# A new order for the front of an attention kernel with a feed-forward behind it: last queries' scores in a score tile, tail keys as 64x64 products, copies changed between two engines, loads by head

## The chip, the cores and the metric

The kernel runs on one core of a Trainium2 chip. The core's engines each run their own queue of instructions in order: TensorE (PE: matrix products; its weight loads are listed as PEld), ScalarE (ACT: functions of single elements, such as the exponential, and copies), VectorE (DVE: element-wise products and copies), GpSimd (POOL: here it issues most loads) and SyncE (SP: here it issues stores, small loads and transposes by DMA). Matrix products write into PSUM, which is cut into banks; ScalarE and VectorE read them from there into SBUF. The metric is the device time of one execution in microseconds, as the median of several runs; lower is better.

## The reference

Attention over 8 batches of 8 heads, 576 positions and 64 dimensions per head, with a bias that depends on the distance of two positions alone, followed by a feed-forward without biases, from 512 to 2048 and back, with a leaky ReLU.

```
scores = scale * (q @ k.T) + bias_table[bucket(|i - j|), head]
attn   = softmax(scores)
x      = (attn @ v)            # (8 * 576) rows x 512
out    = leaky_relu(x @ w_in, 0.01) @ w_out
```

The bucket is constant from a distance of 128 on.

## The kernel before

Two heads make a pair; there are 32 pairs, n = 0 to 31, four to a batch (n_pairs = 4). Every engine's order is the order of the program text (a manual schedule), so the text below is the schedule.

For a pair, q and k are turned (positions from partitions to columns): transpose_q and transpose_k make twelve small PE transposes into a PSUM bank of the pool "m" (two banks), from which a copy writes qt or kt in SBUF. transpose_k also calls apart, which makes a block-diagonal copy of the last 64 keys of both heads. Pairs above 8 are turned by a DMA on SP's queue instead (turn_by_dma), for which pair_rows gathers the rows on VectorE.

Scores are computed with the keys on the partitions, in six units u. Units 0 to 3 (u < NJ) are 128 keys each against the first 512 queries, both heads side by side in a score tile of two banks (pool ps_s, two tiles). Unit 4 (u == NJ) holds those four blocks of keys against the last 64 queries, in the two banks o0 and o1 of the pool ps_o, in which the value products accumulate too. Unit 5 is the last 64 keys (tail keys) of both heads against all 576 queries. qk_mm(n, u) issues the products and exp(n, u, ps) lets ScalarE write the exponentials into at (units 0 to 4) or at4 (unit 5); score(n, u) is both. The maximum isn't subtracted. The bias enters as a factor behind the exponential: band(n, u) multiplies, on VectorE, the columns near the diagonal by rows of hk or hk4, which the program makes at the start from the table (through a row in DRAM, u_row, loaded back by SP's DMAs).

av_tails(n) and av(n, e) multiply with the values, which carry a column of ones, so that the sums stand beside the products; a reciprocal and a product on VectorE give opair. x_transposes(n) turns opair into xT, the input of the feed-forward, by PE and a copy, or by a DMA for later pairs.

The feed-forward works on tiles of 512 rows. ffn_in makes one group: four products of 128x512 into a bank of "m", from which leaky writes gt, on ScalarE in one pass, or, where by_vector is set, on VectorE in two (0.01 times the input into low, then the maximum). ffn_out multiplies back. A planner by counts decides how many groups each pair takes in (plan, groups_of, slot, moe, moe_block). The first tile of 512 rows is complete behind pair 3, so that the first groups stand in the loop of pair 4.

The order around the change: spins (products of zeros, to keep PE occupied), the turns of pair 0, its first scores, then a loop over n = 0 to 3 in which the scores of pair n, the value products of pair n - 1, and the turns of pair n + 1 are interleaved; then pair 4 written out by hand with its first four groups; then one loop over n = 5 to 32. In that loop the tail keys' scores (unit 5) come near the end of a pair, behind nearly all of its groups, and each next pair begins with the products of its units 0 and 1. Loads go through POOL: load_qk(b, h0, h1) is one DMA for q and one for k, load_v_head one head of values, load_v_part one block of 128 positions of several heads, load_v_tail the last 64 positions; loads(n), called from begin(n), issues those that belong to a pair. The values' tiles, q and k of two batches are held at a time.

## Time and profile before

| what | value |
|---|---|
| runs | 377.9, 378.34, 379.27 us (median 378.34) |
| the profiled execution's own time | 378.19 us |
| its span, first to last instruction | 376.4 us |
| TensorE clock granted | 1.0 |
| PE busy | 361.4 us (96%) |
| ScalarE, VectorE, POOL busy | 239.6, 201.8, 77.1 us |
| first feed-forward product | 34.29 us from the span's start |

A row of a timeline gives the start in microseconds, the duration, the engine, the line of the kernel, the operation, "output<-inputs" by the names in the program, partitions x elements, and how many of a kind follow one another (x4); a bracket at its end tells how long the engine stood idle before it, and what ended that. The duration of a merged row is the time that the records cover; since an instruction starts before the record of the one ahead has ended, the distance of two starts is what one takes of the queue. A row of the windows gives a stretch of the span, its length, and the busy time of each engine in it. PE's records are modelled, so that a busy PE need not be at its peak.

### The profile page before, as it was taken

The page shows a single profiled execution, that of the slowest core. Times are in us where ns is not written, and L with a number is a line of the kernel's source. Part 1 is how long each engine was busy: PE and PEld are TensorE (multiplying, and loading weights), DVE is VectorE, ACT ScalarE, POOL GpSimd, SP SyncE. Part 2 cuts the span into 40 slices and gives each one's busy share as a digit, 9 for nine tenths or more (in the row PEclk, how much of TensorE's full clock was granted, in tenths as well). Part 3 has the DMA queues.
Part 4 walks back from the last instruction along what each step waited for, and adds up shares of the span by engine and source line. Part 5 has one row for each costly group of instructions (what it writes and reads, how often), then busy time and mean ns, then how long its engine had stood idle before and what let it go on. Part 6 is the DMA issues. An engine that isn't in the chain of part 4 may idle for free.

```text
span 376.4 us, 8586 instructions
## 1 busy us (share of the span) xinstructions
PE 361.4 (96%) x3501; PEld 186.0 (49%) x3556; DVE 201.8 (54%) x510; ACT 239.6 (64%) x376; POOL 77.1 (20%) x118
## 2 busy tenths in 40 slices
PE   6879999999999999999999999999999999999995
PEld 2455555554455555555545545555555544444442
DVE  4689687777657666666755666655553300200221
ACT  5898777568856787777866666777777255055000
POOL 8772431233023303330323033100000000000000
PEclk9999999999999999999999999999999999999999
DMA  8999999997699959996998699433131000110212
GB/s 104 184 202 182 206 199 136 158 185 121 77 119 157 147 80 125 150 156 84 145 117 127 76 132 117 78 78 78 47 47 45 30 28 2 57 54 2 81 61 84
DMA packets 104352, 40.07 MB, mean 106 GB/s; under 512 B 83184, under 2 KB 98808, under 8 KB 104312
## 3 DMA queue, kind: packets, MB, share of 16 engines
q0 software_dynamic: 53696, 18.36, 47.1%
q1 hardware_dynamic: 50472, 21.02, 28.5%
q8 instruction: 28, 0.46, 0.5%
q10 hardware_dynamic: 144, 0.13, 0.1%
q14 instruction: 12, 0.10, 0.1%
HBM read 37.68 MB, written 9.45 MB: 125 GB/s over the span
## 4 chain that ended last, share of the span: by engine, by line
PE 85%; DMA 4%; ACT 4%; DVE 3%; issue 1%; SPq 1%; another core or an unknown queue 1%; DVEq 0%; ACTq 0%
PE pm L449 32%; PE pm L424 30%; PE ps_o L376 10%; PE ps_s L316 8%; DMA hk<-u_row 3%; PE ps_s L319 1%; PE ps_o L365 1%; ACT at L329 1%; ACT gt L435 1%; DVE opair L380 1%; DMA u_row<-ub 1%; SPq L199 1%; PE ps_tx L398 1%; PE ps_q L309 1%
## 5 line engine op out<-in xcount | busy, mean ns | idle before, releaser
L435 ACT ACTIVATE gt<-pm 128x512 bf16<-128x512 f32 x138 | 82.6, 603 | 88.4 <-PE pm L424 87.5
L424 PE MATMUL pm<-xT,w_in_sb 128*128 128x512 bf16 x543 | 136.4, 379 | 2.0 <-ACT gt L435 0.2
L449 PE MATMUL pm<-w_out_sb,gt 128*128 128x512 bf16 x555 | 130.9, 379 | 1.1
L329 ACT ACTIVATE at<-ps_s 128x1024 bf16<-128x1024 f32 x128 | 124.4, 1030 | 6.9 <-PE ps_s L316 6.8
L352 DVE TENSOR_TENSOR at<-at,hk 128x768 bf16<-128x768 bf16 (+3 forms) x160 | 71.4, 454 | 33.6 <-ACT at L332 19.8
L449 PEld LDWEIGHTS <-gt 128*128 128x128 bf16 x576 | 53.0, 98 | 60.6
L424 PEld LDWEIGHTS <-w_in_sb 128*128 128x128 bf16 x576 | 51.9, 98 | 53.9 <-issue 0.9
L467 DVE COPY y<-pm 128x512 f32<-128x512 f32 x33 | 22.8, 692 | 76.6 <-PE pm L449 76.6
L376 PE MATMUL ps_o<-vn,at 128*128 128x65 bf16 x1280 | 49.6, 194 | 0.0
L376 PEld LDWEIGHTS <-at 128*128 128x128 bf16 x1280 | 44.5, 98 | 9.0 <-issue 0.7
L316 PE MATMUL ps_s<-qt,kt 64*128 64x512 bf16 x256 | 40.4, 381 | 4.5 <-ACT at L329 3.2
L379 DVE RECIPROCAL rcp<-ps_o 128x5 f32<-128x5 f32 x64 | 12.3, 192 | 42.9 <-PE ps_o L376 42.7
L380 DVE TENSOR_TENSOR opair<-ps_o,rcp 128x320 bf16<-128x320 f32 x64 | 31.5, 492 | 3.3
L620 POOL COPY tick<-opair 1x1 bf16<-1x1 bf16 x18 | 4.6, 256 | 134.1 <-DVE opair L380 134.1
L119 POOL DMA_DIRECT2D vn<-in_v_dram x32 | 29.4, 923 | 9.9 <-PE pm L424 3.6
L316 PEld LDWEIGHTS <-kt 64*128 64x128 bf16 x256 | 8.5, 94 | 31.1 <-issue 23.6
L336 ACT ACTIVATE at<-ps_s 128x576 bf16<-128x576 f32 x32 | 21.9, 683 | 0.2 <-PE ps_s L320 0.2
L332 ACT ACTIVATE at<-ps_q 128x256 bf16<-128x256 f32 x64 | 21.6, 403 | 0.5 <-PE ps_q L309 0.4
L459 ACT COPY y<-pm 128x256 f32<-128x256 f32 x1 | 0.4, 372 | 27.5 <-DVE y L459 27.5
L298 DVE COPY kt<-tu 128x576 bf16<-128x576 bf16 x23 | 15.5, 675 | 0.0
L294 DVE COPY qt<-tu 128x576 bf16<-128x576 bf16 x23 | 15.0, 651 | 0.0
L112 POOL DMA_DIRECT2D qn<-in_q_dram x18 | 13.9, 773 | 3.6 <-DMA vn<-in_v_dram 1.0
(59 smaller groups left out, 177.5 us busy)
## 6 DMA issues: line engine op xcount, KB each, us to landing
out_dram<-y SPq DMA_DIRECT2D x35, 256.0 KB, 2.3
qn<-in_q_dram POOLq DMA_DIRECT2D x14, 288.0 KB, 5.5
kn<-in_k_dram POOLq DMA_DIRECT2D x14, 288.0 KB, 6.2
vn<-in_v_dram POOLq DMA_DIRECT2D x28, 128.0 KB, 6.2
w_in_sb<-in_moe_w_in_dram POOLq DMA_DIRECT2D x2, 1024.0 KB, 13.0
w_out_sb<-in_moe_w_out_dram POOLq DMA_DIRECT2D x2, 1024.0 KB, 16.3
qn<-in_q_dram POOLq DMA_DIRECT2D x4, 144.0 KB, 4.1
kn<-in_k_dram POOLq DMA_DIRECT2D x4, 144.0 KB, 4.3
```

The lines of the kernel that those rows point to most:

```text
L119: nc.gpsimd.dma_start(out=vn[b % NBUF][:, c, h0:h1, 0:D], in_=v[b, h0:h1, c * P : (c + 1) * P, :].rearrange("h s d -> s h d"),)
L316: nc.tensor.matmul(ps[:, e, :], lhsT=kt[r, u * P : (u + 1) * P], rhs=qt[r, 0:512], start=True, stop=True)
L329: nc.scalar.activation(at[:, :, u, 0:512], ps, AF.Exp, scale=scale)
L332: nc.scalar.activation(at[:, e, :, 512:S], ps[e][:, 0 : NJ * SL].rearrange("p (c i) -> p c i", i=SL), AF.Exp, scale=scale)
L336: nc.scalar.activation(at4[:, 0:S], ps.rearrange("p e i -> p (e i)")[:, 0:S], AF.Exp, scale=scale)
L352: nc.vector.tensor_tensor(out=o, in0=o, in1=m, op=ALU.mult)
L376: nc.tensor.matmul(ps[:, ic, :], lhsT=at[:, o : o + P], rhs=vn[b % NBUF][:, c, 2 * p + e, :], start=False, stop=(ic == NJ and c == NJ - 1))
L380: nc.vector.tensor_tensor(out=opair[:, :, e * D : (e + 1) * D], in0=ps[:, :, 0:D], in1=rcp.to_broadcast([P, NJ + 1, D]), op=ALU.mult)
L424: nc.tensor.matmul(pm, lhsT=w_in_sb[:, c, f * P : (f + 1) * P], rhs=xT[c][:, t0 : t0 + TT], start=(c == 0), stop=(c == n_cc - 1))
L435: nc.scalar.activation(g, pm, AF.Prelu, bias=0.0, scale=1.0, alpha=0.01)
L449: nc.tensor.matmul(pm, lhsT=gt[:, f, ts * P : (ts + 1) * P], rhs=w_out_sb[:, f, :], start=(f == 0), stop=(f == n_fc - 1))
L467: nc.vector.tensor_copy(out=y, in_=pm)
```

## The change

The loop over pairs 0 to 3 is written anew: pair 0 and the first steps of pair 1 stand ahead of a loop over n = 1 to 3, in which the turns of q and k of the next pair stand together, ahead of the scores of unit 2. For pairs below 4, unit 4 goes to a score tile and is one pass of ScalarE in place of two; unit 5 is made by four products with 64 rows and 64 columns, head by head, and apart isn't called. Copies of q are on ScalarE for pairs 0, 3 and 4 and on VectorE for all others (before: ScalarE for pairs 0 to 4); copies of the turned output are on ScalarE for pairs 0 to 2 (before: VectorE). Values of heads 4 to 7 of batch 0 are loaded head by head, q and k of batch 1 in three parts, of which the last is issued in loads(0), behind the values of batch 1.

In the loop over n = 5 to 32 a branch is added for pairs in which the planner has groups of the first projection alone and fewer than six of them (room["only"]): no group in the second slot, band(n, 1) later, unit 5 ahead of the last two groups, the last bands between the two halves of the group that VectorE finishes. The turns ahead by DMA are a function of their own, turn_ahead, called from begin where the next pair is turned by DMA, and otherwise behind the first value products.

```diff
--- before.py
+++ after.py
@@ -225,10 +225,13 @@
     load_qk(0, 6, H)
     load_v_head(0, 2)
     load_v_head(0, 3)
-    load_qk(1, 0, H // 2)
-    load_v_part(0, range(NJ), 4, H)
+    load_v_head(0, 4)
+    load_v_head(0, 5)
+    load_qk(1, 0, 2)
+    load_v_head(0, 6)
+    load_v_head(0, 7)
     clear_v(nc.gpsimd, 1)
-    load_qk(1, H // 2, H)
+    load_qk(1, 2, 4)
 
     def load_w_in(half):
         o = slice(half * (DF // 2), (half + 1) * (DF // 2))
@@ -290,17 +293,33 @@
 
     def transpose_q(n):
         qt = qts[n] = qt_pool.tile([P, S], BF16, name="qt")
-        copy = nc.scalar.copy if n <= n_pairs else nc.vector.tensor_copy
+        copy = nc.scalar.copy if n == 0 or n_pairs - 1 <= n <= n_pairs else nc.vector.tensor_copy
         copy(out=qt[:, 0:S].rearrange("p (r c) -> p r c", c=NC), in_=turned_pair(n, 0))
 
     def transpose_k(n):
         kt = kts[n] = kts_[n % 2]
         nc.vector.tensor_copy(out=kt[:, 0:S].rearrange("p (r c) -> p r c", c=NC), in_=turned_pair(n, 1))
-        apart(kt)
+        if n >= n_pairs:
+            apart(kt)
 
     def qk_mm(n, u):
 
         qt, kt = qts[n], kts[n]
+        if n < n_pairs and u >= NJ:
+            ps = ps_s_pool.tile([P, 2, 512], FP32, name="ps_s")
+            if u == NJ:
+                for c in range(NJ):
+                    for e in range(2):
+                        r = slice(e * D, (e + 1) * D)
+                        nc.tensor.matmul(ps[:, e, c * SL : (c + 1) * SL], lhsT=kt[r, c * P : (c + 1) * P],
+                                         rhs=qt[r, 512:S], start=True, stop=True)
+                return ps
+            for half, cols in ((0, slice(0, 512)), (1, slice(512, S))):
+                for e in range(2):
+                    r = slice(e * D, (e + 1) * D)
+                    nc.tensor.matmul(ps[e * SL : (e + 1) * SL, half, 0 : cols.stop - cols.start],
+                                     lhsT=kt[r, NJ * P : S], rhs=qt[r, cols], start=True, stop=True)
+            return ps
         if u == NJ:
             ps = [ps_o_pool.tile([P, 512], FP32, name="ps_q", tag=f"o{e}") for e in range(2)]
             for c in range(NJ):
@@ -327,6 +346,10 @@
         at, at4 = at_view(n), at4_[n % 2]
         if u < NJ:
             nc.scalar.activation(at[:, :, u, 0:512], ps, AF.Exp, scale=scale)
+        elif u == NJ and n < n_pairs:
+            nc.scalar.activation(at[:, :, :, 512:S],
+                                 ps[:, :, 0 : NJ * SL].rearrange("p e (c i) -> p e c i", i=SL),
+                                 AF.Exp, scale=scale)
         elif u == NJ:
             for e in range(2):
                 nc.scalar.activation(at[:, e, :, 512:S],
@@ -396,7 +419,8 @@
         ps = ps_m_pool.tile([P, 8 * P], BF16, name="ps_tx", tag="m")
         for ic in range(NJ + 1):
             nc.tensor.transpose(ps[:, ic * P : (ic + 1) * P], in_=opair[:, ic, :], identity=ident)
-        nc.vector.tensor_copy(out=xT[p][:, b * S : (b + 1) * S], in_=ps[:, 0:S])
+        copy = nc.scalar.copy if n < n_pairs - 1 else nc.vector.tensor_copy
+        copy(out=xT[p][:, b * S : (b + 1) * S], in_=ps[:, 0:S])
 
 
     gts = {}
@@ -425,11 +449,13 @@
                              start=(c == 0), stop=(c == n_cc - 1))
         return pm
 
-    def leaky(T, f, pm, by_vector=False):
+    def leaky(T, f, pm, by_vector=False, between=None):
         g = gts[T][:, f, :]
         if by_vector:
             low = low_pool.tile([P, TT], BF16, name="low")
             nc.vector.tensor_scalar(low, pm, 0.01, None, op0=ALU.mult)
+            if between is not None:
+                between()
             nc.vector.tensor_tensor(out=g, in0=low, in1=pm, op=ALU.max)
         else:
             nc.scalar.activation(g, pm, AF.Prelu, bias=0.0, scale=1.0, alpha=0.01)
@@ -521,16 +547,19 @@
         keep = min(n_fc, 4 * ((n - 1) // n_pairs)) if more <= N else 0
         return max(4, min(8, (have - keep) // (more - n)))
 
-    room = {"left": 0, "lead": False, "split": False, "keep": 0}
+    room = {"left": 0, "lead": False, "split": False, "only": False, "keep": 0}
 
     def plan(n):
         g = room["left"] = groups_of(n)
         room["lead"] = can("out") and g >= 8 and not can("in")
         room["split"] = can("out") and g < 8 and not can("in")
+        room["only"] = can("in") and not can("out") and g < 6
         room["keep"] = 4 if can("out") and not room["lead"] else 0
 
     def slot(second=False):
 
+        if room["only"] and second:
+            return
         if room["split"]:
             if second:
                 piece_out()
@@ -610,6 +639,7 @@
             load_w_in(0)
             load_v_part(1, range(NJ))
             load_v_tail(1)
+            load_qk(1, H // 2, H)
             load_w_in(1)
             load_w_out(0)
         elif n == 2:
@@ -632,6 +662,10 @@
         loads(n)
         if n_pairs + 1 < n + 1 < N and not by_dma(n + 1):
             pair_rows(n + 1)
+        if by_dma(n + 1):
+            turn_ahead(n)
+
+    def turn_ahead(n):
         for m in range(n + 2, min(n + AHEAD + 1, N)):
             if by_dma(m) and m - (AHEAD if m > 2 * n_pairs + 2 else 2) == n:
                 pair_rows(m)
@@ -646,39 +680,43 @@
     spin(2)
     score(0, 0)
     score(0, 1)
-    for n in range(n_pairs):
-        begin(n)
+    begin(0)
+    score(0, 2)
+    transpose_k(1)
+    transpose_q(1)
+    spin(3)
+    score(0, 3)
+    spin(3)
+    score(0, 5)
+    score(0, 4)
+    score(1, 0)
+    score(1, 1)
+    begin(1)
+    transpose_k(2)
+    spin(3)
+    for u in (0, 1, 2, 5, 4):
+        band(0, u)
+    score(1, 2)
+    transpose_q(2)
+    score(1, 3)
+    for n in range(1, n_pairs):
         if n > 1:
+            begin(n)
             band(n - 1, 5)
             band(n - 1, 4)
-        if n == 1:
-            for u in (0, 1, 2, 5, 4):
-                band(0, u)
-        if n == 0:
+            transpose_k(n + 1)
+            transpose_q(n + 1)
             score(n, 2)
-        transpose_k(n + 1)
-        if n < 2:
-            spin(3)
-        if n > 0:
-            score(n, 2)
-        if n == 1:
+        av_tails(n - 1)
+        av(n - 1, 0)
+        band(n, 0)
+        if n > 1:
             score(n, 3)
-        if n > 0:
-            av_tails(n - 1)
-            av(n - 1, 0)
-            band(n, 0)
-        if n != 1:
-            score(n, 3)
-        if n > 0:
-            av(n - 1, 1)
-        transpose_q(n + 1)
-        if n < 1:
-            spin(3)
+        av(n - 1, 1)
+        band(n, 1)
         score(n, 5)
-        if n > 0:
-            band(n, 1)
-            x_transposes(n - 1)
-            band(n, 2)
+        band(n, 2)
+        x_transposes(n - 1)
         score(n, 4)
         score(n + 1, 0)
         score(n + 1, 1)
@@ -722,13 +760,15 @@
             exp(n, 1, ps_b)
         av_tails(n - 1)
         av(n - 1, 0)
+        if live and not by_dma(n + 1):
+            turn_ahead(n)
         if live:
             band(n, 0)
         if more:
             transpose_q(n + 1)
         slot()
         av(n - 1, 1)
-        if live:
+        if live and not room["only"]:
             band(n, 1)
         if more:
             transpose_k(n + 1)
@@ -744,7 +784,24 @@
             finished(n - 1)
         if not live:
             break
+        if room["only"]:
+            band(n, 1)
         band(n, 2)
+        if room["only"]:
+            exp(n, 3, ps_b)
+            moe(2)
+            exp(n, 4, ps_c)
+            score(n, 5)
+            T, f = step("in")
+            room["left"] -= 1
+
+            def last_bands():
+                band(n, 5)
+                band(n, 4)
+
+            leaky(T, f, ffn_in(T, f), True, last_bands)
+            moe(room["left"])
+            continue
         block = moe_block()
         next(block)
         exp(n, 3, ps_b)
```

## The prediction

> **What bounds the kernel now.** I read the granted clock and the page's table of 40 slices first, then the windows of the front, then the timelines of ScalarE (ACT), VectorE (DVE) and TensorE (PE) there. The clock is 1.0 throughout, so no term below is a clock term.
>
> ```profile
> span 376.4 us, 8586 instructions
> PE 361.4 (96%) x3501; PEld 186.0 (49%) x3556; DVE 201.8 (54%) x510; ACT 239.6 (64%) x376; POOL 77.1 (20%) x118
> PE   6879999999999999999999999999999999999995
> ACT  5898777568856787777866666777777255055000
> PEclk9999999999999999999999999999999999999999
> ...
> 12.35:18.54 6.19, 5.04 (x98) 3.21 (x99) 4.93 (x14) 5.36 (x8) 4.21 (x8) 1.00 1.37 209
> 18.54:24.13 5.59, 4.50 (x105) 3.06 (x103) 4.56 (x13) 5.33 (x8) 2.83 (x4) 1.00 1.62 197
> 24.13:29.64 5.51, 4.55 (x107) 3.16 (x104) 4.55 (x13) 5.38 (x9) 4.11 (x6) 1.00 1.18 211
> 38.68:47.13 8.45, 8.24 (x105) 4.83 (x107) 5.68 (x13) 6.41 (x10) 3.18 (x5) 1.00 1.25 206
> 47.13:56.16 9.03, 8.41 (x106) 4.85 (x107) 7.19 (x18) 7.04 (x12) 3.24 (x5) 1.00 1.38 200
> ```
>
> Each window row gives its length, then the busy time of PE, weight loads, VectorE, ScalarE and POOL. Over the span PE is the bound, but not in the front: in the pairs that run from 18.54 and 24.13 ScalarE is busy 5.33 of 5.59 and 5.38 of 5.51 us, PE only 4.5. From pair 5 (38.68) on PE has 8.24 of 8.45. So a microsecond won or lost in the ScalarE-bound front moves everything behind it; once the change's stretch ends, at 56 us, the same PE work follows at its own pace, and nothing there absorbs a shift.
>
> ```profile
> 12.70 3.82 ACT L329 ACTIVATE at<-ps_s 128x1024 bf16<-128x1024 f32 x4
> 17.14 0.64 ACT L294 COPY qt<-ps_t 128x576 bf16<-128x576 bf16 x1 [0.63 <-PE ps_t L279]
> 17.68 0.66 ACT L336 ACTIVATE at<-ps_s 128x576 bf16<-128x576 f32 x1
> 18.74 0.66 ACT L332 ACTIVATE at<-ps_q 128x256 bf16<-128x256 f32 x2 [0.40 <-PE ps_q L309]
> 19.28 3.78 ACT L329 ACTIVATE at<-ps_s 128x1024 bf16<-128x1024 f32 x4
> 23.13 0.64 ACT L294 COPY qt<-ps_t 128x576 bf16<-128x576 bf16 x1
> 23.66 0.66 ACT L336 ACTIVATE at<-ps_s 128x576 bf16<-128x576 f32 x1
> 24.39 0.66 ACT L332 ACTIVATE at<-ps_q 128x256 bf16<-128x256 f32 x2
> 24.93 3.78 ACT L329 ACTIVATE at<-ps_s 128x1024 bf16<-128x1024 f32 x4
> 30.44 3.78 ACT L329 ACTIVATE at<-ps_s 128x1024 bf16<-128x1024 f32 x4
> ```
>
> Starts give what each operation really takes of the queue: a 128x1024 exponential (23.13-19.28)/4 = 0.96 us, a 576-wide q copy 23.66-23.13 = 0.53, the two 256-wide ones 24.93-24.39 = 0.54, a 576-wide exponential about the copy's 0.55. From one pair's first exponential to the next are 6.58 us (pair 1), 5.65 (pair 2) and 5.51 (pair 3).
>
> **The change part by part.** (1) ScalarE's work. Q copies 1 and 2 leave it, q copies 3 and 4 stay; output copies of pairs 0, 1 and 2 come to it, in pair loops 1, 2 and 3. Both kinds are 576 wide from PSUM, so I price an output copy at the q copy's 0.53. The last queries' scores become one pass of 512 elements: half of a 1024-wide one, 0.48 instead of 0.54. Loop 2 then costs 4 x 0.96 + 0.53 + 0.55 + 0.53 + 0.48 = 5.93 us against 5.65, loop 3 5.93 against 5.51: **+0.28 and +0.42**, with ScalarE without a pause. Their waits of before go: the new order hands PE the next scores early, and each score tile is free one exponential (0.96) before it is needed. But this is work on the engine that binds there.
>
> (2) Loop 1, where VectorE takes over.
>
> ```profile
> 13.11 1.36 DVE L352 TENSOR_TENSOR at<-at,hk 128x512 bf16<-128x512 bf16 x3 [2.98 <-DMA hk<-u_row]
> 14.79 0.66 DVE L352 TENSOR_TENSOR at<-at,hk 128x192 bf16<-128x192 bf16 x2 [0.32 <-ACT at L329]
> 15.37 0.75 DVE L298 COPY kt<-ps_t 128x576 bf16<-128x576 bf16 x1
> 16.15 0.23 DVE L286 TENSOR_TENSOR kt<-kt,own 128x128 bf16<-128x128 bf16 x1
> 16.30 0.19 DVE L379 RECIPROCAL rcp<-ps_o 128x5 f32<-128x5 f32 x1
> 17.48 0.49 DVE L380 TENSOR_TENSOR opair<-ps_o,rcp 128x320 bf16<-128x320 f32 x1
> ...
> 12.67 0.45 PE L279 MATMUL ps_t<-ident,kn 96*64 96x96 bf16 x12
> 18.03 0.45 PE L398 MATMUL ps_tx<-ident,opair 128*128 128x128 bf16 x5 [0.63 <-DVE opair L380]
> ```
>
> Before, VectorE does pair 0's five band products as soon as their DMA lands (13.11), then the k copy of pair 2, and ends pair 0's output at 17.48 + 0.49 = 17.97; PE's output transposes (18.03) wait for it, and in PE's order the scores behind them. After, the k copy stands first, the bands second, a q copy of 0.75 (priced as the k copy) third. The k copy follows its transposes. They are issued behind products that now wait for score tiles: exponential (0,3) starts about 10.6 instead of 10.1 (12.70 less 0.54, 0.55, 0.53 and 0.96), since the q transposes (0.45) now stand ahead of its product; then 0.96 + 0.55 + 0.48 and some 0.2 for a tile's turn give exponential (1,0) at about 12.8 (12.70 before, though a q copy is gone). PE's products of (1,0) and (1,1) wait for those tiles, which puts the k transposes at about 13.04 against 12.67, and the copy at 13.5. Then 13.5 + 0.78 (k copy, 16.15-15.37) + 2.02 (bands, 1.36+0.66) + 0.75 (q copy) + 1.67 (from 16.30 to 17.97) = 18.72, **0.75 later** than 17.97. Queued behind that are the output transposes, ScalarE's output copy (0.53, new there), exponential (1,4), and pair 2's first. From 18.72: transposes from 18.76 to 19.25, copy until 19.8, 0.48, so pair 2's first exponential at about 20.3 against 19.28: **+1.0**. ScalarE would idle some 1.3 us ahead of exponential (1,5), whose product now stands behind pair 0's delayed value products, and 0.7 ahead of the copy. Bounds: if none of that idling came, loop 1 would be 4 x 0.96 + 0.55 + 0.53 + 0.48 = 5.40 us, 1.18 less than the 6.58 of before; above, nothing in the rows reaches past 1.4 (the k copy behind the bands' last, 0.40 more). I take +1.0, the sum along the chain.
>
> A fast loop 1 would be stopped soon anyway:
>
> ```profile
> 12.31 10.10 DMA hk<-u_row
> ```
>
> This row of the chain of waits is the load of the last four heads' band rows, landing at 22.4; pair 2's first band product needs it, and VectorE's queue has pair 1's outputs behind that.
>
> (3) Pair 4, up to the first feed-forward group, keeps its code. Its first exponential moves from 30.44 by 1.0 + 0.28 + 0.42 = 1.7 to 32.1. Pair 3's exponential (3,4) now shares the two score tiles, so PE issues pair 4's second product later, and pair 3's value products behind it: **+0.2** (0, if ScalarE's wait covers it; 0.4, the 576-wide tile's turn, at most).
>
> (4) Loops 5 and 6. Only these two take the new branch: the counts give first-projection work alone and fewer than six groups there, and seven or eight in every later pair. Each keeps its five groups, four through ScalarE and one through VectorE, but the last tail-key product moves ahead of the last two groups.
>
> ```profile
> 47.13 0.39 PE L316 MATMUL ps_s<-qt,kt 64*128 64x512 bf16 x2
> 47.92 0.39 PE L316 MATMUL ps_s<-qt,kt 64*128 64x512 bf16 x2 [0.40 <-ACT at L336]
> 56.16 0.39 PE L316 MATMUL ps_s<-qt,kt 64*128 64x512 bf16 x2
> 56.95 0.39 PE L316 MATMUL ps_s<-qt,kt 64*128 64x512 bf16 x2 [0.40 <-ACT at L336]
> ```
>
> Twice the next pair's second product waits 0.40 for the late tail exponential: it starts 0.79 after the first, 0.5 more than the 0.22 or so in which the two follow each other elsewhere. Both go: **-1.0**. Bounds: 0, and the PE idle of the windows, 0.21 + 0.62, with 0.47 at the start of pair 7, -1.3. VectorE's bands sit between the two halves of its group, which holds one of the two "m" banks longer (0.25 + 0.45 us); I cover that with the group behind it (0.87 of PE work).
>
> (5) Tail keys as 64x64 products. Four matmuls in place of two; the two heads sit in different rows and columns of the array. The block-diagonal product (0.23, on VectorE) goes for pairs 1 to 3. I price PE at 0, nearest row:
>
> ```profile
> 16.98 0.39 PE L319 MATMUL ps_s<-qt,kt 128*128 128x512 bf16 x1
> 17.20 0.19 PE L320 MATMUL ps_s<-qt,kt 128*128 128x64 bf16 x1
> ```
>
> The second starts 0.22 behind the first. Were the heads to run one after the other, each tail tile would be 0.24 later; in loop 1 that falls on the path, in loops 2 and 3 it fits the quarter microsecond that PE leads ScalarE. So 0 to +0.4; a gain only on VectorE, already in (2). The Trainium skill, "TensorEngine Tiling (Array Packing)", Key Properties, says that a change of tiling mode drains the array. It would set a drain ahead of and behind each of these products; by it I would be at the upper end. The rows show 64-row score products between 128-row ones already, without a gap of their own.
>
> (6) Loads. The number of POOL's DMAs ahead of the first half of w_in stays 22 (two of q and k less wide, heads 4 to 7 of batch 1 moved behind the values of batch 1).
>
> ```profile
> 20.79 0.75 POOL L235 DMA_DIRECT2D w_in_sb<-in_moe_w_in_dram  x1 [1.23 <-DMA qn<-in_q_dram]
> 32.11 0.90 POOL L239 DMA_DIRECT2D w_out_sb<-in_moe_w_out_dram  x1 [3.87 <-DMA w_in_sb<-in_moe_w_in_dram]
> 34.29 1.02 PE L424 MATMUL pm<-xT,w_in_sb 128*128 128x512 bf16 x3
> 46.17 1.03 PE L424 MATMUL pm<-xT,w_in_sb 128*128 128x512 bf16 x4
> ```
>
> POOL's last row waits for the DMA eight issues before it: the first half lands near 32.1, used at 34.29. After, it stands behind fewer bytes and lands earlier; the second half has the same bytes ahead as before, two issues more, and its first use (the ninth group, 46.17 before) comes no sooner than before. Price 0; without that cover, a late second half would stop PE for what it is late. The moved turn of pair 9 (a transpose on SP's queue) is issued one output product and its neighbours later in loop 7 and read in loop 8, a whole loop of nine us or more behind: 0.
>
> **Sum.** 1.0 + 0.28 + 0.42 + 0.2 - 1.0 = +0.9 us on the profiled execution's own 378.19 us, span 376.4 and 1.8 around it. That lies 0.15 under the median of 378.34. I predict 379.1.
>
> **Rivals.** A, slower: the new branch of loops 5 and 6 returns nothing. Place: the two "m" banks. With no group between the k transposes and the scores, the block's first group must wait for the k copy (0.75, behind the output product) and the next for the xT copy; at the end the bank under the split VectorE group stays taken until bands and maximum are done. It decides once these waits reach 0.5 us per loop; then -1.0 becomes 0, and with 0.2 of (5) the time is 378.19 + 2.1 = 380.3. For it: VectorE has 7.19 of 9.03 us there. Against: output product and k copy (0.49 + 0.75) take VectorE little longer than the scores and output transposes ahead of that group take PE (some 1.1), so I expect 0.2. B: the band load at 22.4, not VectorE's chain, sets pair 3's first exponential, at 22.4 + 2.5 (as before, 24.93), so parts (1) for loop 2 and (2) cost nothing: 0.42 + 0.2 - 1.0 = -0.4, 377.8. It needs loop 1 to idle under 0.5 us. C: ScalarE runs through loop 1 at 5.40 and the band load, behind fewer early bytes, lands a microsecond sooner: -1.18 + 0.28 + 0.42 - 1.3 = -1.8, with pair 4's own waits (0.2 for a group's bank) -2.0: 376.2. Only that drops below the bound of no change. D: the change does all it says, and the front loses 2 us by ScalarE while loops 5 and 6 gain 1: the forecast.
>
> **Chances.** Two measurements of this kernel tell 0.5%, 1.9 us, from nothing: faster is below 376.4, slower above 380.2. Forecast 0.52 (378.3 to 380.2; nearly all within the bound, 0.03 above), A 0.24 (0.20 above), B 0.14 (within), C 0.10 (0.09 below). So faster 0.09, same 0.68, slower 0.23. The range for 8 in 10 leaves out C's centre and A's far end: 377.2 to 380.9.
>
> **What would show it.** Right: exponential (2,0) at 20 to 20.5, ScalarE idle of about 2 us in loop 1 and none in loops 2 and 3, periods of 5.9 there; first feed-forward product at 36 to 36.5; no PE wait on the 576-wide exponential at pairs 6 and 7. Wrong: exponential (2,0) by 19.3; loops 5 and 6 longer than 8.5 us with PE waiting for VectorE; PE waiting for a DMA of w_in, q, k or v; tail-key products over 0.6 us apart from their exponential. The forecast fails if ScalarE's copies prove cheaper than 0.53, or if VectorE starts the bands by 13.5.

## The result and the profile after

| | before | after |
|---|---|---|
| median of 9 executions each (us) | 378.34 (377.9 to 379.34) | 379.73 (379.36 to 381.08) |
| ratio, 95% interval | | 1.0037 (1.002 to 1.0054) |
| profiled execution's own time, span (us) | 378.19, 376.4 | 379.51, 377.6 |
| first feed-forward product (us) | 34.29 | 36.04 |

The kernel became slower by 1.4 us, or 0.37%; the interval leaves out no change, and its upper end is just over the 0.5% within which the prediction counted a difference as none. 379.1 was predicted.

The page of the changed kernel: span, busy times, and of the table of 40 slices the row of TensorE's granted clock.

```profile
span 377.6 us, 8593 instructions
PE 362.6 (96%) x3509; PEld 186.8 (49%) x3564; DVE 201.3 (53%) x505; ACT 240.2 (64%) x373; POOL 77.7 (21%) x120
...
PEclk9999999999999999999999999999999999999999
```

Totals hardly moved: PE has 1.2 us more, VectorE 0.5 less, ScalarE 0.6 more. Where the time went can be read only pair by pair. ScalarE's timeline in the front (start, duration, engine, line, operation; L348 the 128x1024 exponentials, L359 the tail keys', L423 the output copy):

```profile
13.10 3.88 ACT L348 ACTIVATE at<-ps_s 128x1024 bf16<-128x1024 f32 x4
18.19 0.65 ACT L359 ACTIVATE at<-ps_s 128x576 bf16<-128x576 f32 x1 [1.22 <-PE ps_s L320]
19.44 0.64 ACT L423 COPY xT<-ps_tx 128x576 bf16<-128x576 bf16 x1 [0.60 <-PE ps_tx L421]
...
20.46 1.95 ACT L348 ACTIVATE at<-ps_s 128x1024 bf16<-128x1024 f32 x2
22.27 0.67 ACT L297 COPY qt<-ps_t 128x576 bf16<-128x576 bf16 x1
22.79 2.00 ACT L348 ACTIVATE at<-ps_s 128x1024 bf16<-128x1024 f32 x2
24.61 0.73 ACT L359 ACTIVATE at<-ps_s 128x576 bf16<-128x576 f32 x1
...
26.21 1.99 ACT L348 ACTIVATE at<-ps_s 128x1024 bf16<-128x1024 f32 x2
...
31.99 3.90 ACT L348 ACTIVATE at<-ps_s 128x1024 bf16<-128x1024 f32 x4
```

The windows of loops 1 and 2 and of loops 5 and 6 (length, then busy time of PE, weight loads, VectorE, ScalarE, POOL, then clock, DMA share, GB/s):

```profile
13.10:20.46 7.36, 5.46 (x102) 3.31 (x102) 5.96 (x15) 5.54 (x8) 4.55 (x9) 1.00 1.64 208
20.46:26.21 5.75, 4.75 (x99) 3.19 (x99) 4.04 (x10) 5.75 (x10) 5.75 (x9) 1.00 1.11 168
...
40.43:48.91 8.48, 8.30 (x104) 4.96 (x107) 5.32 (x13) 7.15 (x11) 1.99 (x3) 1.00 1.26 204
48.91:57.61 8.70, 8.46 (x105) 5.00 (x107) 6.96 (x18) 7.15 (x11) 2.95 (x5) 1.00 1.42 199
```

The account, from the distances of the same events in both traces:

| stretch | before | after | difference | predicted |
|---|---|---|---|---|
| start, up to pair 1's first exponential | 12.70 | 13.10 | +0.40 | +0.1 |
| loop 1 | 6.58 | 7.36 | +0.78 | +1.0 with the start |
| loop 2 | 5.65 | 5.75 | +0.10 | +0.28 |
| loop 3 | 5.51 | 5.78 | +0.27 | +0.42 |
| pair 4, to the first feed-forward product | 3.85 | 4.05 | +0.20 | +0.20 |
| pair 5, from its value products to the next pair's | 9.03 | 8.48 | -0.55 | -0.5 |
| pair 6, the same | 9.02 | 8.69 | -0.33 | -0.5 |
| pair 7, the same | 9.03 | 9.44 | +0.41 | 0 |

(Value products of a pair are here those that stand in its turn of the loop.) The differences add up to 1.28; the two executions' own times differ by 1.32. From pair 8 on the shift stays at 1.28 to the last product, so nothing behind absorbs it.

The first row of the table isn't the change's doing as far as the traces show. The 0.40 arises ahead of pair 0's first exponential (7.23 before, 7.63 after; from there to pair 1's first both take 5.47), in code that the change leaves as it was. PE's opening spins and the turn of q behind them ran slower there for longer: nine spins took 3.57 us before and 4.02 after, with no wait for a load ahead of the turn of q, and that turn 0.45 and 0.69.

```profile
1.23 3.57 PE L598 MATMUL ps_w<-junk 128*128 128x512 bf16 x9 [1.23 <-DVE junk L146]
```

```profile
1.22 4.02 PE L627 MATMUL ps_w<-junk 128*128 128x512 bf16 x9 [1.22 <-DVE junk L146]
```

In all 14 traces pair 0's first exponential stands between 7.18 and 7.71, early and late in both orders. So 0.40 of the 1.28 is chance; without it the two traces would differ by 0.88. The medians differ by more, and single traces don't tell what makes up the rest.

In loops 2 and 3 ScalarE runs without a pause (5.75 busy of 5.75), but in less than the 5.93 predicted. In loop 1 it waits 1.22 and 0.60 us, close to the 1.3 and 0.7 predicted. What stands behind those waits is in VectorE's and PE's timelines of that loop:

```profile
13.97 0.76 DVE L301 COPY kt<-ps_t 128x576 bf16<-128x576 bf16 x1 [3.03 <-PE ps_t L282]
14.64 1.92 DVE L375 TENSOR_TENSOR at<-at,hk 128x512 bf16<-128x512 bf16 x5
16.48 0.75 DVE L297 COPY qt<-ps_t 128x576 bf16<-128x576 bf16 x1
17.21 0.20 DVE L402 RECIPROCAL rcp<-ps_o 128x5 f32<-128x5 f32 x1
...
18.40 0.49 DVE L403 TENSOR_TENSOR opair<-ps_o,rcp 128x320 bf16<-128x320 f32 x1
```

```profile
16.39 1.40 PE L399 MATMUL ps_o<-vn,at 128*128 128x65 bf16 x40
17.72 0.43 PE L320 MATMUL ps_s<-qt,kt 64*64 64x512 bf16 x4
18.95 0.45 PE L421 MATMUL ps_tx<-ident,opair 128*128 128x128 bf16 x5 [0.80 <-DVE opair L403]
```

The k copy of pair 2 runs first (13.97), the bands of pair 0 behind it until 16.56. Pair 0's value products (16.39) need the bands, the tail product (17.72) stands behind them, and the output transposes wait until 18.95 for VectorE. The q copy (16.48) lies in the chain only if the reciprocal waited for it rather than for the products; both end near 17.2, and this trace can't tell which.

### The profile page after: what moved, and what is told of

The parts are those of the page before. It is cut to its first block, busy times and chain, and to the rows that moved or that the text cites. A ratio compares the mean times of both kernels' runs of the same rounds, so it can differ in the third digit from the quotient of the medians.

```text
span 377.6 us, 8593 instructions
## 1 busy us (share of the span) xinstructions
PE 362.6 (96%) x3509; PEld 186.8 (49%) x3564; DVE 201.3 (53%) x505; ACT 240.2 (64%) x373; POOL 77.7 (21%) x120
## 4 chain that ended last, share of the span: by engine, by line
PE 84%; DVE 5%; ACT 4%; DMA 3%; issue 2%; another core or an unknown queue 1%; SPq 0%; DVEq 0%; ACTq 0%
PE pm L475 32%; PE pm L448 31%; PE ps_o L399 9%; PE ps_s L335 7%; DVE at L375 2%; ACT at L348 2%; PE ps_s L338 2%; DMA hk<-u_row 2%; PE ps_o L388 1%; DMA u_row<-ub 1%; PE ps_q L328 1%; DVE qt L297 1%; DVE opair L403 1%; ACT gt L461 1%
## 5 line engine op out<-in xcount | busy, mean ns | idle before, releaser
L348 ACT ACTIVATE at<-ps_s 128x1024 bf16<-128x1024 f32 x128 | 124.8, 1030 | 8.5 <-PE ps_s L335 8.5
L119 POOL DMA_DIRECT2D vn<-in_v_dram x28 | 26.2, 943 | 6.1 <-PE ps_s L339 3.5
L359 ACT ACTIVATE at<-ps_s 128x576 bf16<-128x576 f32 x32 | 22.0, 689 | 1.6 <-PE ps_s L320 1.2
L355 ACT ACTIVATE at<-ps_q 128x256 bf16<-128x256 f32 x56 | 18.9, 406 | 0.2 <-ACT gt L461 0.2
```

The lines of the kernel that those rows point to most:

```text
L119: nc.gpsimd.dma_start(out=vn[b % NBUF][:, c, h0:h1, 0:D], in_=v[b, h0:h1, c * P : (c + 1) * P, :].rearrange("h s d -> s h d"),)
L348: nc.scalar.activation(at[:, :, u, 0:512], ps, AF.Exp, scale=scale)
L355: nc.scalar.activation(at[:, e, :, 512:S], ps[e][:, 0 : NJ * SL].rearrange("p (c i) -> p c i", i=SL), AF.Exp, scale=scale)
L359: nc.scalar.activation(at4[:, 0:S], ps.rearrange("p e i -> p (e i)")[:, 0:S], AF.Exp, scale=scale)
```

## The experiments

Shifts below are those of pair 4's and pair 8's value products against the trace of before (after: +1.76 and +1.28). Where the mean granted clock of an execution fell under 0.997 (below), the median of the others, called undisturbed, is given too: 379.60 for after (6 of 9), 378.40 for before (84 of 93 measured beside the experiments). By these the schedule costs 1.2; leaving out the executions with a fallen clock lowers the median of after by 0.13 and that of the 93 by 0.05. The 93 were measured in three batches, with undisturbed medians of 378.18, 378.42 and 378.46, so differences of 0.2 or 0.3 between runs of different batches say nothing.

**The front alone, and the branch alone.** e1 takes the branch of loops 5 and 6 out of the changed kernel and puts the turns ahead back to a pair's beginning; e2 is the kernel before with that branch alone.

```
e1:  room["only"] = False
     def begin(n): ...
-        if by_dma(n + 1):
-            turn_ahead(n)
+        turn_ahead(n)
     (and the call of turn_ahead behind av(n - 1, 0) taken out)
e2:  before, with room["only"], the early return of slot, band(n, 1) moved,
     leaky(..., between) and the block  if room["only"]: ... continue
```

> The new front with pairs 5 and later as before. Theory from the two profiles: the new branch of pairs 5 and 6, with the moved turn, gave back about 0.5 us, so without it this run is 380.2, 0.5 above the changed kernel, and its first feed-forward product stands 1.3 to 1.8 us later than 34.29. Rival (the prediction's own price): the branch gave back 1.0, so 380.7. Rival 2: it gave nothing, 379.7.

> The kernel before with the new branch of pairs 5 and 6 alone, the turns ahead left in begin. Theory: 0.5 us gained against before, 377.8; the PE wait for the tail exponential is gone, and in its place PE waits for VectorE, where pair_rows of the pair after next stands behind the split group. Rival: the full 1.0, 377.3. Rival 2: nothing, 378.3.

e1: 381.4 us (ratio 1.0064, 1.0046 to 1.0082); the two of its six executions with an undisturbed clock have a median of 380.33, 1.9 above before. The predicted front, 1.0 + 0.28 + 0.42 + 0.2, is 1.9, but two executions are few, and the trace of after has 1.75 up to pair 4, 0.40 of it from its late start. The profiled execution itself shows something else. Its windows (columns as above) and one row of ScalarE:

```profile
20.00:22.00 2.00, 1.37 (x26) 1.07 (x25) 0.82 (x2) 2.00 (x4) 1.22 (x2) 0.75 1.50 164
22.00:24.00 2.00, 2.00 (x36) 1.57 (x32) 0.43 (x1) 1.87 (x3) 2.00 (x3) 0.50 1.04 130
24.00:26.00 2.00, 1.69 (x29) 0.90 (x26) 1.62 (x5) 1.23 (x2) 2.00 (x4) 0.90 1.09 204
```

```profile
24.66 1.02 ACT L348 ACTIVATE at<-ps_s 128x1024 bf16<-128x1024 f32 x1 [0.79 <-PE ps_s L335]
```

The granted clock falls to half for some 3 us right behind loop 1. PE falls behind, ScalarE waits 0.79 for it, and loop 2 takes 7.20 us in place of 5.75.

e2: 378.18 (0.9998, 0.9983 to 1.0013). In its trace the shift falls from 0.89 at pair 4 to 0.32 at pair 8, by 0.57: the branch returns about half of the 1.0 on the old front as well, so the new front isn't what limits it. The medians show less: 0.08 between e2 and the executions of before beside it, with an interval that holds both 0 and some 0.5. Its 0.89 ahead of the branch comes with unchanged code: the start is 0.39 late, and pair 0's bands wait for their rows. VectorE's row, and ScalarE's first exponential of pair 2:

```profile
14.47 2.02 DVE L352 TENSOR_TENSOR at<-at,hk 128x512 bf16<-128x512 bf16 x5 [3.95 <-DMA hk<-u_row]
```

```profile
20.32 1.95 ACT L329 ACTIVATE at<-ps_s 128x1024 bf16<-128x1024 f32 x2
```

The rows landed at 14.47 here, at 13.11 in the profile of before, and at 12.86 to 13.56 in the other three traces of the old front. With a late landing the old loop 1 takes 20.32 - 13.09 = 7.23 us, only 0.13 less than the new one.

**Loop 1 and ScalarE's copies.** Three edits of the changed kernel, each with a different link: e4 puts the bands ahead of the k copy, e8 the q copies back on ScalarE, e3 the output copies back on VectorE.

```
e4:      begin(1)
+        for u in (0, 1, 2, 5, 4):
+            band(0, u)
         transpose_k(2)
         spin(3)
-        for u in (0, 1, 2, 5, 4):
-            band(0, u)
e8:  -   copy = nc.scalar.copy if n == 0 or n_pairs - 1 <= n <= n_pairs else nc.vector.tensor_copy
     +   copy = nc.scalar.copy if n <= n_pairs else nc.vector.tensor_copy
e3:  -   copy = nc.scalar.copy if n < n_pairs - 1 else nc.vector.tensor_copy
     +   copy = nc.vector.tensor_copy          (of the turned output)
```

> The changed kernel with pair 0's band products ahead of the k copy of pair 2. Theory: VectorE's chain in loop 1 starts with the band rows' landing instead of the k copy; pair 2's first exponential comes 0.5 to 0.8 us earlier, 379.1. Rival: the chain is set by PE or ScalarE (the wait for score tiles) and the order of two VectorE operations changes under 0.2 us: 379.6.

> The changed kernel with q copies 1 and 2 on ScalarE again. Theory: loop 1's chain is VectorE's (k copy, bands, q copy, output of pair 0), so without the q copy of 0.7 pair 2's first exponential comes 0.4 to 0.7 earlier, although ScalarE has 1.06 more to do, since it idles 1.8 us there: 379.2. Rival: ScalarE's work is the bound, and the time rises by 0.5: 380.2.

> The changed kernel with all output copies on VectorE. Theory: ScalarE binds loops 2 and 3, so each loses about 0.45 us of period (from 5.75 to 5.3), and loop 1 some 0.1 to 0.5: 378.4. Rival: VectorE's chain (bands, k copy, outputs) sets the period as soon as it has the copy of 0.45 again: gain under 0.4, 379.4.

e8: 379.82 (1.0034, 1.0017 to 1.0051), like after and neither of the two expected. VectorE's row behind the bands:

```profile
17.21 0.20 DVE L402 RECIPROCAL rcp<-ps_o 128x5 f32<-128x5 f32 x1 [0.65 <-PE ps_o L399]
```

Without the q copy the reciprocal starts at the same 17.21 and now waits 0.65 for PE's value products; pair 2 begins at 20.46 again. So the q copy wasn't on the chain in after.

e4: 379.52 (1.0033, 1.0015 to 1.0051); 379.42 undisturbed, 0.2 under after, too little to tell. VectorE's timeline, and pair 2's first exponential:

```profile
13.21 1.36 DVE L375 TENSOR_TENSOR at<-at,hk 128x512 bf16<-128x512 bf16 x3 [2.30 <-DMA hk<-u_row]
...
15.52 0.75 DVE L301 COPY kt<-ps_t 128x576 bf16<-128x576 bf16 x1
```

```profile
20.10 1.95 ACT L348 ACTIVATE at<-ps_s 128x1024 bf16<-128x1024 f32 x2
```

Loop 1 falls from 7.36 to 20.10 - 13.07 = 7.03 us: the place of the k copy ahead of the bands cost 0.33. The shift at pair 4 is 1.38, yet at pair 8 it is 2.37. The loss has its own cause, in pair 8, in the rows of VectorE and PE:

```profile
72.71 0.65 DVE L297 COPY qt<-tu 128x576 bf16<-128x576 bf16 x1 [3.08 <-DMA tu<-pr]
```

```profile
74.04 0.29 PE L328 MATMUL ps_q<-qt,kt 64*128 64x64 bf16 x7 [1.20 <-DVE opair L403]
```

Pair 9's turn by DMA (tu) landed late, VectorE stood 3.08 us before its copy, and PE 1.20 behind VectorE. Such waits are in the traces of e3, e6, b1, b2, b3 and r1 too (0.69 to 2.11 us), with the turn issued at either place, and in neither of the traces of before and after. They lengthened pair 8, which takes 10.21 us otherwise, by 1.40 in e4, 0.44 in e6, 0.24 in e3 and 0.23 in b1, and not at all in b2, b3 and r1. How often it happens in all executions can't be said from single profiles.

e3: 379.49 (1.0038, 1.002 to 1.0056). ScalarE's first exponentials of pairs 2, 3 and 4:

```profile
20.16 1.93 ACT L348 ACTIVATE at<-ps_s 128x1024 bf16<-128x1024 f32 x2
...
25.65 1.93 ACT L348 ACTIVATE at<-ps_s 128x1024 bf16<-128x1024 f32 x2
...
31.14 3.84 ACT L348 ACTIVATE at<-ps_s 128x1024 bf16<-128x1024 f32 x4
```

Loops 2 and 3 take 5.49 us each, less than before's 5.65 and 5.51, and loop 1 loses 0.30. The output copies on ScalarE therefore cost 0.30 + 0.26 + 0.29 = 0.85 up to pair 4. At pair 8 some 0.5 of it is left (+0.79 against +1.28), the rest going to pair 6, which takes 8.88 in place of 8.69, and to the late turn in pair 8. The undisturbed median, 379.42, is only 0.18 under after and near the rival's 379.4, so the 0.85 is shown by the trace and not by the medians.

**The units of pairs 1 to 3.** e7 makes the last queries' and the tail keys' scores as before (two passes of 256, block-diagonal tail keys with apart) in the new order.

```
e7:  -   if n < n_pairs and u >= NJ: ...      (score tile, 64x64 products)
     -   elif u == NJ and n < n_pairs: ...    (one pass of ScalarE)
     -   if n >= n_pairs:
     -       apart(kt)
     +   apart(kt)
```

> The changed kernel with units 4 and 5 of pairs 0 to 3 as before: two banks and two ScalarE passes, and 128-wide tail products with the block-diagonal copy on VectorE. Theory: the products themselves change nothing (prediction's price 0 for the 64x64 form), ScalarE gains 0.06 per pair back and the score tiles are less shared, VectorE has 0.23 more per pair; first feed-forward product within 0.4 of the changed kernel's, 379.7. Rival: the 64x64 form costs a drain of the array, and without it PE's wait is shorter by 0.3 in each loop: 379.0.

e7: 379.84 (1.0037, 1.0015 to 1.006), 379.81 undisturbed. Its one profile is 0.67 ahead of after at pair 8 (0.45 of it by pair 1's first exponential), the twelve executions are not ahead at all. So the new units cost nothing that the medians can show. The traces do show two small costs. Pair 4, up to the first feed-forward product, takes 35.37 - 31.50 = 3.87 in e7, as before (3.85), against 4.05 in after. And a 64x64 tail product starts later behind 128-wide products than a 128x128 one does. The rows behind three spins, before and after:

```profile
10.45 0.82 PE L598 MATMUL ps_w<-junk 128*128 128x512 bf16 x3
11.11 0.38 PE L319 MATMUL ps_s<-qt,kt 128*128 128x512 bf16 x1
```

```profile
10.74 0.82 PE L627 MATMUL ps_w<-junk 128*128 128x512 bf16 x3
11.49 0.43 PE L320 MATMUL ps_s<-qt,kt 64*64 64x512 bf16 x4
```

The distance is 0.66 before and in e7, and 0.75 in after. Behind pair 0's value products in loop 1 it is 17.01 - 15.77 = 1.24 in e7 and 17.72 - 16.39 = 1.33 in after: 0.09 more both times. Behind turns, in b2, it isn't longer (0.38, as before).

**The branch's other half.** e5 copies the rows of the pair after the next in the middle of the pair, behind exponential 3, in place of its beginning; b1 is e2 with the same edit, on the old front.

```
     def begin(n):
-        if n_pairs + 1 < n + 1 < N and not by_dma(n + 1):
+        if n_pairs + 1 < n + 1 < N and not by_dma(n + 1) and n + 1 not in prs:
             pair_rows(n + 1)
     if room["only"]:
         exp(n, 3, ps_b)
+        if not by_dma(n + 2):
+            pair_rows(n + 2)
         moe(2)
```

> The changed kernel with pair_rows of the pair after next moved, in the new branch, behind the third band product, where VectorE stands idle 1.5 us. Theory: what the new branch gives back late (PE waits for those rows and for the q copy behind them, 0.2 in pair 6 and 0.4 in pair 7) goes: 0.4 to 0.6 us less, 379.1, and pair 8 starts that much earlier against pair 4 than in the changed kernel. Rival: those PE waits come from the split group's maximum itself: under 0.1 changes, 379.7.

> The kernel before with the new branch of pairs 5 and 6 and the rows of the pair after next gathered early, the front as before. Theory: the branch gives 0.5 (as in the run with the branch alone) and the early rows 0.4 more: 377.5, 0.9 below before; the wait of pair 7 for the q copy's bank is gone. Rival: the rows were only a symptom, and it stays at the 378.0 of the branch alone.

b1: **377.19** (0.9966, 0.9953 to 0.9979; five executions), under both kernels; b3 below, the same with two spins, has 377.37 over twelve. e5: 379.3 (1.0023, 1.0005 to 1.0041), 379.24 undisturbed, 0.36 under after. Between pairs 4 and 8 the shift falls by 0.76 in e5 and by 0.88 in b1 (1.11 without the late turn in pair 8), against 0.48 in after. Pair by pair:

| | pair 5 | pair 6 | pair 7 |
|---|---|---|---|
| before | 9.03 | 9.02 | 9.03 |
| after | 8.48 | 8.69 | 9.44 |
| e5, r1 | 8.48 | 8.46 | 9.38 |
| b1, b2, b3 | 8.48 | 8.46 | 9.03 |

So the branch is worth 0.55 in each of its two pairs, 1.1 in all, and the rest is lost again behind it. PE's timeline in pair 7 of after, and VectorE's first copy of rows and q copy there:

```profile
58.30 0.77 PE L399 MATMUL ps_o<-vn,at 128*128 128x65 bf16 x20
59.05 0.43 PE L278 MATMUL ps_t<-ident,pr 96*128 96x96 bf16 x6
...
61.02 0.42 PE L278 MATMUL ps_t<-ident,pr 96*128 96x96 bf16 x6
61.54 1.02 PE L448 MATMUL pm<-xT,w_in_sb 128*128 128x512 bf16 x4
```

```profile
58.64 0.35 DVE L260 COPY pr<-qn 96x768 bf16<-96x768 bf16 x1
...
60.74 0.74 DVE L297 COPY qt<-ps_t 128x576 bf16<-128x576 bf16 x1
```

The same of b1:

```profile
56.51 0.77 PE L376 MATMUL ps_o<-vn,at 128*128 128x65 bf16 x20
57.12 0.42 PE L275 MATMUL ps_t<-ident,pr 96*128 96x96 bf16 x6
...
59.09 0.41 PE L275 MATMUL ps_t<-ident,pr 96*128 96x96 bf16 x6
59.34 1.03 PE L424 MATMUL pm<-xT,w_in_sb 128*128 128x512 bf16 x4
```

```profile
58.41 0.75 DVE L294 COPY qt<-ps_t 128x576 bf16<-128x576 bf16 x1
```

In b1 the turn of q follows the start of the value products by 0.61 us, as it did before. In after it stands 0.75 behind, right at the end of the copy of the rows that it reads (58.64 + 0.35 = 58.99); in pair 6 it stands 0.83 behind (50.43), where that copy ends at 50.37. The group shown last follows its transposes by 0.25 in b1, as before, and by 0.52 in after: it starts as the q copy ends (60.74 + 0.74 = 61.48), which by the program frees the bank of "m" that this group takes, and VectorE has ended the split group and made four copies of rows ahead of it. These three delays, 0.22, 0.14 and 0.27, are each too short to be bracketed as a wait, and together they are the 0.6 that the branch didn't return in after.

In e5 pair 8's rows are early, but pair 9's, which the moved turn puts behind the first value products, still stand ahead of the q copy (61.05 to 61.66, the copy at 61.92), and pair 7 takes 9.38. In b1 the turn is issued at the pair's beginning, the q copy ends at 59.16, before its group, and pair 7 takes 9.03. So with the rows early the moved turn costs 0.35; b2 and b3 agree with b1, and r1 with e5, but no run moves the turn alone.

**The clock.** e6 adds three spins (products of zeros) to loop 1 of the changed kernel, b3 two to loop 1 of b1.

```
         score(n, 5)
+        if n == 1:
+            spin(3)          (b3: spin(2))
```

> The changed kernel with three spins (products of zeros) in loop 1 behind the products of unit 5, where PE stands idle about 1 us. Theory: that gap is what lets the granted clock fall to a half for one window in about every third execution (mean clock 0.995, about 1 us longer); with the gap filled nearly all executions have a clock of 0.998 or more, the median falls to 379.5 and the spread narrows; the profile's schedule is otherwise the same. Rival: the clock falls for other reasons (as in 4 of 41 executions of the old front), and as many executions as before show 0.995.

> As the first of these runs, with two spins behind the products of unit 5 in loop 1. Theory: the clock falls in the old front too, rarely (about one execution in ten), by the same gap; with spins none of 12 executions is below 0.997, the median is the same within 0.2. Rival: the spins delay the output transposes and cost 0.3 or more in every execution.

e6: 379.63 (1.0019, 1.0003 to 1.0034); all twelve between 379.18 and 380.23, and none with a clock under 0.997. b3: 377.37 (0.9977, 0.9964 to 0.9991), one of twelve under. So in the new order the fallen clock was rarer with spins, in the old order (12 of 122 without them, below) it wasn't, and the middle stays where it was: spins are no cure for the schedule's 1.2.

**Parts joined.** b2 is b1 with q copies from pair 3 on on VectorE and the 64x64 tail products for pairs below 4. r1 is the changed kernel with the edits of e3, e4, e5, e6 and e8.

> As the run before, with q copies 3 and 4 on VectorE in place of ScalarE and the 64x64 tail products without the block-diagonal copy in pairs 0 to 3. Theory: ScalarE binds loops 2 and 3 of the old front, so without 0.53 there each period falls from 5.5 to about 5.2 (VectorE then has 5.1): 0.5 less than the run before, 377.0. Rival: VectorE's chain, longer by the q copy, sets the period: no gain, or 0.3 more.

> The changed kernel with what the runs found against it undone: output copies on VectorE, pair 0's bands ahead of the k copy, q copies up to 4 on ScalarE, rows early, three spins in loop 1. Theory: loops 2 and 3 fall from 5.75 to 5.5, loop 1 by 0.5 or more, the branch gives 0.4 more: 378.0, no slower than before. Rival: the new order itself (turns of k and q together, unit 4 in the score tiles) costs what is left: 379.0.

b2: 378.84 (1.0013, 1.0 to 1.0026), 1.7 above b1, a loss that neither the expectation nor its rival had in this size. The tail keys' exponential in loop 3 (the one in loop 2 waits as long):

```profile
29.68 0.65 ACT L345 ACTIVATE at<-ps_s 128x576 bf16<-128x576 f32 x1 [0.43 <-PE ps_s L310]
```

A q copy taken from ScalarE (0.53) becomes a wait of 0.43 there: its next exponential waits for the tail product, which stands behind the turns in PE's order. Loop 3 is at 5.50 and loop 2 at 6.01 (5.51 and 5.65 before), and pair 4, up to the first feed-forward product, takes 4.34 in place of 3.85. So in the old order the q copy was nearly free on the engine that binds; b2 changes the tail products as well, and the two weren't tried apart.

r1: 378.03 (1.0005, 0.9979 to 1.0032). Its loop 1 is 6.54, loops 2 and 3 are 5.50 and 5.48: the front is back where it was (6.58, 5.65, 5.51), and its trace gains 0.77 between pairs 4 and 8. It is 0.8 above b1 by the medians. Pair 7, 9.38 as in e5, can be 0.35 of this; the rest isn't settled, since its one profile is its fastest execution (377.3), and three of its twelve lie above 381.

## Why the prediction was right, point by point

**What bounds.** The shift made in the front went through to the end, and nothing behind pair 8 absorbed any of it.

**(1) Loops 2 and 3.** ScalarE ran without a pause, and e3 shows that the output copies make the difference. The size was too large: 5.93 predicted, 5.75 and 5.78 measured. The term at fault is the 0.96 of a 1024-wide exponential, taken from (23.13 - 19.28)/4. That distance also holds a wait too short for a bracket: the copy at 23.13 follows PE's turn of q, whose record ends at 23.04.

```profile
22.59 0.45 PE L279 MATMUL ps_t<-ident,qn 96*64 96x96 bf16 x12
```

The record of the four was 3.78 before, and the mean of one is 1.03, so that the step is (3.78 - 1.03)/3 = 0.917. In after, two take 22.27 - 20.46 = 1.81 and 24.61 - 22.79 = 1.82, so the four take 3.63 in place of 3.84. The other passes took 0.03 more than priced in loop 2 and 0.06 more in loop 3, which leaves the error: 0.18 and 0.15. The Trainium skill, "ScalarE: Activation LUTs", section "What ACT_TABLE_LOAD costs", says that back-to-back activations overlap by about 93 ns; by it the step would be an estimated 1.03 - 0.09 = 0.94, nearer than 0.96, and the trace shows an overlap of 0.11 to 0.13 (1.03 less 0.917, and less 1.81/2).

**(2) Loop 1.** Place and size were right: the k copy ahead of the bands, ScalarE's two waits (1.22 and 0.60), exponential (2,0) at 20.46, in the predicted 20 to 20.5. One link was wrong: the sum had the q copy's 0.75 on the chain, and e8 shows that the value products take that stretch anyway, so that this alone changed nothing in the sum. The sum came out near because two other errors met. The k copy was at 13.97, not 13.5, with 0.30 of this from pair 1's first exponential at 13.10 and not 12.8; and the k copy and the bands behind it took 0.67 and 1.84 of VectorE's queue, not 0.78 and 2.02. Pair 0's output ended at 18.40 + 0.49 = 18.89, against 18.72. The late start is the chance told above: with the old order that exponential stood at 12.70 in before, 13.09 in e2 and 12.73 in b1, and I count it to neither side. Without it loop 1 lost 0.78 where the sum had 0.9. Not foreseen was that the old loop 1 depends on a landing that varies: 6.58 with the rows at 13.11, 7.23 at 14.47. The new one doesn't, since its k copy ends at 14.7 anyway, and takes 7.36 in after, e1, e5, e6 and e8.

**(3) Pair 4:** +0.20, as predicted, and for the reason given: with unit 4 back in its own banks, in e7, the stretch takes 3.87, as before.

**(4) Loops 5 and 6.** The two waits of 0.40 on the tail exponential went, as predicted, and each of the two pairs gave 0.55 (the 0.79 of the prediction's rows less its 0.22 is 0.57). But 0.48 of 1.0 arrived at pair 8. The step that was wrong is the cover: what VectorE does later was to be hidden by the group behind it, at no cost. It cost 0.22 in pair 6 and 0.41 in pair 7, and rival A came true by half. Its engine, VectorE, was right, and its place, the "m" banks, for 0.27 of this; the rest is PE waiting for the rows themselves. The work that delays VectorE is one that neither the forecast nor the rival named: copies of rows, 0.35 us each, four of them in pair 7 between the split group and the q copy. With two of them moved ahead, the branch returns 0.76 in e5 and 1.11 in b1; b1's median returns 378.40 - 377.19 = 1.2. The 1.0 was there to be had. The second window, 8.70 us from 48.91, is also past the 8.5 that the prediction named as a sign of being wrong.

**(5) 64x64 products at 0:** the four take PE 0.43 us, the two of before 11.52 - 11.11 = 0.41, so the heads don't run one after the other. A change of tiling does show, as the 0.09 told under e7. In loop 1 it is on the path: the tail exponential starts 18.19 - 16.39 = 1.80 behind the value products in after, and 17.45 - 15.77 = 1.68 in e7. That lies in the stated 0 to 0.4, near its lower end; the price of 0 was a little low.

**(6) Loads and the moved turn at 0:** no PE wait for a load in after. In e1 and e4 PE waited 0.36 and 0.21 for pair 1's k, which is issued ahead of all that the change moves. The loads by head weren't tried alone. The moved turn landed in time in after, but the rows that move with it are not free on VectorE: 0.35 in pair 7, by e5 against b1. And pair 9's turn, late in some traces, is a transfer of the stretch that can stop PE.

**No clock term:** the profile of after agrees, its executions don't quite: three of nine have a mean granted clock of 0.995, 380.3 to 381.08 us. The forecast lacked this term, 0.13 us of after's median.

The errors have opposite signs: 0.33 too much in loops 2 and 3, 0.5 too little loss in the branch, a start late by chance and the clock on top. 379.1 was near 379.73 partly by luck in their sum. What the experiments bear out singly is pair 4's 0.2, the output copies as the cost in loops 2 and 3, and the place of loop 1's loss; the front's 1.9 rests on two executions of e1.

## What to carry to other kernels

A distance of two starts may hold a wait too short to be listed: take a repeated operation's step from the record of the row, (record of N less the last one's) / (N - 1). A copy is dear on the engine that binds a stretch and nearly free where that engine would wait anyway, so look at what the engine would wait for next before moving it. When a reordering takes away a wait and only half of it returns, look at the starts of the same products behind it: delays of 0.14 to 0.27 us, unlisted, had eaten the rest, and moving one deferred piece of work (the rows) to a place where its engine stood idle brought it back in the old front, and less than half of it in the new.

## What was not expected of the hardware

The granted clock fell to half for one short stretch in some executions. In e1's profile PE was busy 1.37 of 2 us in the window from 20 (and 1.04 of the 2 us ahead of it); the clock in the windows from 20, 22 and 24 was 0.75, 0.50 and 0.90. The lost clock, 0.25 x 2 + 0.50 x 2 + 0.10 x 2 = 1.7 us, is that of some 3.4 us at half. The longest idle times of PE listed from 18 us on were 0.80 and 0.79 us (the first stands in after's row at 18.95). The Trainium skill, "TensorE: Matmul & The Clock Gate", has two rules that bear on this: "HAM oscillation" has the clock halved after a gap of over some 3.4 us, "A second HAM failure mode: psum-queue depth-cycling" by short idle times between groups, if there are many. No such long gap was there; the trace agrees with the second rule rather than the first, in a stretch of a few microseconds. The same windows of after have the same PE busy times (1.04 and 1.37) and a clock of 1.00, so such gaps don't always bring the fall. It stands in e5's trace too, with 0.71, 0.50 and 0.94 in these windows. Executions with a mean clock under 0.997 were 18 of 75 in the new order without spins, 1 of 24 in the new order with spins, and 12 of 122 in the old order without them. That the gaps of loop 1 are the cause is what the spins suggest; it wasn't shown by a kernel that changes the gaps alone, since spins also give PE work, and in the old order b3 with spins had one such execution in twelve, as many as without.

The opening of the kernel varies too. The turn of q behind the first spins took 0.69 us in after and 0.45 in before, and turns of the same kind took 0.68 and 0.69 in e1 from 20.95, where the granted clock was falling to a half. Spins start 0.43 us apart at first and 0.22 later. So PE's first microseconds seem to run at half speed, up to a moment that varies, though the profile's clock reads 1.00 there.

Landings vary from execution to execution without a change of the code: the band rows between 12.86 and 14.47 us, pair 9's turn from no wait to 3.08 us. One profile each can hold more than half a microsecond of such luck, more than several of the edits were worth.
